# A planner that no longer charges the matmul behind a turn, and new priorities for every stage

## The chip, the cores and the metric

The kernel runs on one core of one Trainium2 chip. The metric is the device time of one execution in microseconds (us). Three runs of the kernel before gave 891.21, 891.24 and 893.26 us, so the median is 891.24 us. Engines are named as the profile names them: PE is TensorE (PEld its weight load), DVE is VectorE, ACT is ScalarE, POOL is GpSimd, SP is SyncE, which issues most DMAs.

## The reference: what is computed

Attention of 4 batches with 8 heads each (sequence 1152, head size 64), with the queries averaged in pairs, followed by a low-rank mix over the sequence and an MLP with a residual:

```python
q_pool = q.reshape(B, H, S // 2, 2, D).mean(axis=3)            # 576 queries per head
scores = q_pool @ k^T / sqrt(D); attn = softmax(scores)
x = (attn @ v) -> [4, 576, 512]
u = x + ((x^T @ U) @ V)^T                                       # U [576, 32], V [32, 576]
out = u + relu(u @ w_ch1) @ w_ch2                               # 512 -> 2048 -> 512
```

The weights of the second part arrive as 64-bit floats and are decoded on the chip.

## The kernel before, in words

The program is not written in the order in which it runs. The functions `head(n)` (32 heads) and `tail(b, clock)` (4 batches) record operations into a `Plan` with `op(at, ways, r, w, ...)`: `at` is a priority (a due time in ns), `ways` names the engines that may do it and a cost in ns on each, `r` and `w` are the buffers read and written. `Plan.run` then goes through all operations once, always giving the next free engine the earliest startable operation in order of due time, and emits the instructions in the order found. The costs and due times therefore decide only the order on each engine, the buffer slots and, for operations recorded with `dual` (L404), whether DVE or POOL does them. On the chip the engines then run these fixed queues with semaphores between them.

A head consists of these steps (lines of the kernel before):

- Loads of q, k, v by SP; the pooled query `qp` (L528, a dual operation); for batches 0 and 1 a split of k into a rounded half and the rest (L541 on ACT, L542 dual).
- Turns: transposes on PE into a PSUM bank of the pool `m` (5 banks): `qT` (L552, 3 fp32 transposes), `kT` (L630, 3 fp32r transposes, three such operations for a head of batches 0 and 1), or for batches 2 and 3 `kTw` (L585: one operation of 4 and one of 1 fp32 transposes).
- Scan: 14 matmuls per head (L657 of 384 columns, L659 of 288) into `m` banks, each followed by a DVE maximum over the bank (L663). The row maxima (L668) are turned by `mT` (L686, one fp32r transpose).
- Scores: 18 pairs of matmuls (L717 and L718) into the pool `s` (3 banks), exponentials on ACT (L724), and 7 or 8 sums of the exponentials into `acc` (L700, dual).
- `value` (L749: 18 matmuls with fp32 operands, each shown as two records) and, for each second head, the total of the exponentials (`total`, L740) and the turns `t2`, `t4` (L773) and `t3` (L786).

A batch's tail is the mix (L832, L851, additions L853), turns of u (`tu`, L923, 4 fp32 transposes per block of rows, split into halves by ACT L932 and DVE L933), and the MLP: first layer L957, second layer L1072, additions into X on DVE (L1076). For the last batch the first layer is done with 7 products instead of 8 (`pair`, L1001) and its operands are made at L897 to L914. MLP matmuls are spread between the heads of the next batch by their due times (`MLP_START`, `MLP_RATE`); the first batch's weights are decoded on ACT, DVE and POOL (L433 to L441) and split (L882, dual).

The planner marks the operations that are turns, value products or totals as `short` (a name for "not one of the plain one-pass matmuls"). Its rule `TURN` says that a matmul that is not `short` starts 82 ns later if the operation before it on PE was `short`.

Of the kernel before, what the change touches and what calls it, by code (L numbers as in the profile page):

```python
# [10 lines left out]
F32R = mybir.dt.float32r  # L11
# [27 lines left out]
class Op:  # L39
    __slots__ = ("at", "ways", "bufs", "deps", "succ", "open", "way", "start", "end", "seq", "port", "short")  # L40


class Plan:
# [12 lines left out]
    TURN = 82.0  # L56
# [4 lines left out]
    def op(self, at, ways, r=(), w=(), port=False, short=False):  # L61

        o = Op()
        o.short = short
# [27 lines left out]
    def run(self, slack, bias, bias_from, link):  # L92
# [9 lines left out]
        lead = False  # L102
# [42 lines left out]
        def pick(e):  # L145

            found, first = [], None
            for at, seq, base, o in cand[e][:self.WINDOW]:
                t = max(base, free[e] + (self.TURN if lead and e == "pe" and not o.short else 0.0))
# [37 lines left out]
        while len(order) < len(self.ops):  # L187
# [15 lines left out]
            if e == "pe":  # L203
                lead = o.short
# [34 lines left out]
def kernel(  # L239
# [33 lines left out]
    QT, KS = -9.86, -10.24  # L273
    LEAD = 60000.0, 9000.0
# [4 lines left out]
    TSW, TOT, TSL = 257.0, 235.0, -108.0  # L279
    SUM, AV, YT = 0.8, 0.51, 0.8184  # L280
# [3 lines left out]
    KT, MX0, MXS = 0.79, -8.744, 3.819  # L284
# [120 lines left out]
    TP, TPR, MOVE = 89, 84, 130  # L405
# [107 lines left out]
    def head(n):  # L513
        op = plan.op if n < len(heads) - 4 else lambda at, ways, r=(), w=(), port=False, short=False: plan.op(at, ways, [*r, *arena], w, port, short)
# [39 lines left out]
        op(T(QT), ("pe", 194, qT), [qp, (Q1, "use"), (Q2, "use")], [pt], short=True)  # L554
# [21 lines left out]
        def turn_whole(part, j0, j1):  # L576
# [11 lines left out]
            op(at, ("pe", len(kt_blocks) * TP if len(kt_blocks) > 1 else 27, kT), [(kt, 0), (T1, "use")], [pt_], short=True)  # L588
# [34 lines left out]
        else:  # L623
            for c in range(3):
# [7 lines left out]
                op(T(QT + KT * c), ("pe", 262, kT), kk[c] + [(T1, "use")], [pt_], short=True)  # L632
# [15 lines left out]
        for p0, p1 in ((0, 3), (3, 5)) if n == 0 else ((0, 5),):  # L648
# [23 lines left out]
            if n == 0:  # L672
# [4 lines left out]
                op(at, ("pe", np_ * TPR, mT), [mx], [pt2], short=True)  # L677
# [8 lines left out]
            op(at, ("pe", 62, lambda mx=mx, pt2=pt2, np_=np_: nc.tensor.transpose(  # L686
                pt2.t[0:np_, 0:P].bitcast(F32R), mx.t[:, 0:np_], identr)), [mx], [pt2], short=True)
# [14 lines left out]
        for j in range(NJ):  # L702
            if j % 2 == 0:
                pair_ = j + 1 < NJ
                pu[j] = new("p2" if pair_ else "p1")
                if pair_:
                    pu[j + 1] = pu[j]
                    todo = [((j, j + 1), 0, NARROW, j), ((j,), NARROW, NQ, j + 0.9), ((j + 1,), NARROW, NQ, j + 1.441)]
                else:
                    todo = [((j,), 0, HALF, j), ((j,), HALF, NQ, j + 0.4171)]  # L710
# [438 lines left out]
```

## Time and profile before

| | |
|---|---|
| median of 3 runs | 891.24 us |
| the profiled execution | 891.29 us |
| its span in the trace | 889.5 us |
| granted PE clock over the span | 1.00 (2.4 GHz) |
| PE busy | 880.7 us (99%) |
| DVE busy | 733.5 us (82%) |
| ACT busy | 521.4 us (59%) |
| POOL busy | 224.1 us (25%) |

The profiled execution took 891.29 us, of which 1.79 us lie around the span. Busy PE time is made of overlapping records: each matmul is shown for longer than the distance to the next start. A late start is therefore read from the distance between two starts in the timeline, not from the busy share.

### The profile page before, as it was taken

Reading aid. Unit: us, or ns where it says so; the run is one execution under the profiler, and the core shown is the slowest. Engines: PE = TensorE matmul, PEld = TensorE weight load, DVE = VectorE, ACT = ScalarE, POOL = GpSimd, SP = SyncE. Lnnn points to the kernel's source line nnn. Section 1 sums busy time; section 2 is a strip of 40 time slices with the busy share of each in tenths; the row PEclk is TensorE's granted clock in tenths of the full one; section 3 lists DMA queues with packets and bytes.
Section 4 is the critical chain, followed back from the end, with each engine's and each line's share of the span. In section 5 each row is a group of like instructions: output and inputs, shape, how many; then the busy total and the mean of one; then the engine's idle time right before and its main releaser. Section 6 shows DMA issues by size and latency. Waiting matters only on the chain.

```text
span 889.5 us, 15636 instructions
## 1 busy us (share of the span) xinstructions
PE 880.7 (99%) x5597; PEld 723.2 (81%) x5597; DVE 733.5 (82%) x1481; ACT 521.4 (59%) x1183; POOL 224.1 (25%) x224
## 2 busy tenths in 40 slices
PE   9999999999999999999999999999999999999998
PEld 8787777778787777889888888888888778899987
DVE  8899999988999989968786778787875554798885
ACT  6788889847787787655554657556564321322221
POOL 3323334434433455330213121200102000101110
PEclk9999999999999999999999999999999999999999
DMA  6244346345576664433332332324242255565432
GB/s 173 76 131 139 107 149 203 92 158 194 186 230 208 204 206 159 152 100 110 105 112 81 112 93 89 112 80 120 85 115 101 95 172 189 176 202 188 166 102 102
DMA packets 63635, 124.00 MB, mean 139 GB/s; under 512 B 5931, under 2 KB 33350, under 8 KB 63558
## 3 DMA queue, kind: packets, MB, share of 16 engines
q1 hardware_dynamic: 62214, 118.46, 41.2%
q10 hardware_dynamic: 1344, 4.56, 2.0%
q8 instruction: 44, 0.72, 0.4%
q14 instruction: 33, 0.27, 0.1%
HBM read 96.17 MB, written 21.50 MB: 132 GB/s over the span
## 4 chain that ended last, share of the span: by engine, by line
PE 87%; DVE 10%; ACT 1%; DMA 1%; issue 1%; POOL 0%; SPq 0%; DVEq 0%; POOLq 0%; ACTq 0%
PE m L1072 21%; PE m L957 16%; PE m L749 15%; PE s L717 7%; PE s L718 7%; PE m L657 7%; PE s L1001 6%; DVE mp L663 4%; DVE acc L700 2%; PE m L740 1%; PE m L630 1%; PE m L773 1%; PE m L585 1%; PE m L659 1%; PE m L552 1%; PE m L923 1%
## 5 line engine op out<-in xcount | busy, mean ns | idle before, releaser
L724 ACT ACTIVATE big<-s 128x320 f32<-128x320 f32 (+2 forms) x448 | 202.2, 479 | 104.9 <-PE s L718 101.2
L663 DVE TENSOR_REDUCE mp<-m 128x1 f32<-128x384 f32 (+1 forms) x448 | 214.5, 533 | 21.2 <-PE m L657 20.2
L1072 PE MATMUL m<-w,hh 128*128 128x512 f32 x798 | 221.2, 395 | 0.2 <-DVE XH L796 0.2
L957 PE MATMUL m<-rest,w 128*128 128x512 f32 (+1 forms) x768 | 180.5, 354 | 0.6 <-DVE mp L663 0.4
L717 PE MATMUL s<-room 128*128 128x256 f32 (+2 forms) x576 | 166.6, 301 | 0.3 <-ACT big L724 0.3
L1072 PEld LDWEIGHTS m<-w,hh 128*128 128x128 f32 x798 | 144.5, 188 | 25.8 <-DVE XH L796 0.4
L718 PE MATMUL s<-room 65*128 65x256 f32 (+2 forms) x576 | 164.5, 297 | 0.4 <-DMA room<-mr 0.4
L749 PE MATMUL m<-big,v 128*64 128x288 f32 x1152 | 148.5, 410 | 0.6 <-ACT mr L688 0.6
L957 PEld LDWEIGHTS m<-rest,w 128*128 128x128 f32 x768 | 131.5, 188 | 15.6 <-issue 1.3
L700 POOL TENSOR_TENSOR acc<-acc,big 128x576 f32<-128x576 f32 x67 | 95.7, 1428 | 156.1 <-ACT big L724 62.2
L700 DVE TENSOR_TENSOR acc<-acc,big 128x576 f32<-128x576 f32 x149 | 115.1, 773 | 13.2 <-ACT big L724 10.9
L657 PE MATMUL m<-room 128*128 128x384 f32 x384 | 124.7, 357 | 1.3 <-DVE mp L663 0.5
L749 PEld LDWEIGHTS m<-big,v 128*64 128x64 f32 x1152 | 79.1, 137 | 57.1 <-issue 2.1
L717 PEld LDWEIGHTS s<-room 128*128 128x128 f32 x576 | 109.0, 189 | 9.6 <-issue 2.2
L718 PEld LDWEIGHTS s<-room 65*128 65x128 f32 x576 | 108.9, 189 | 5.8 <-issue 0.5
L657 PEld LDWEIGHTS m<-room 128*128 128x128 f32 x384 | 69.3, 189 | 15.4 <-DVE mp L663 4.2
L1076 DVE TENSOR_TENSOR X<-m,X 128x512 f32<-128x512 f32 x95 | 64.7, 684 | 16.9 <-PE m L1072 16.6
L961 ACT ACTIVATE hh<-m 128x512 fp32r<-128x512 f32 (+1 forms) x64 | 33.0, 515 | 70.2 <-PE m L957 66.1
L397 ACT ACTIVATE room<-m 64x288 fp32r<-64x288 f32 (+1 forms) x173 | 72.4, 427 | 2.7 <-PE m L552 0.4
L963 DVE SCALAR_TENSOR_TENSOR hh<-m,hh 128x512 fp32r<-128x512 f32 (+1 forms) x64 | 37.5, 586 | 32.4 <-ACT hh L961 32.0
L565 POOL CAST qb<-room 64x64 fp32r<-64x64 f32 x57 | 17.5, 308 | 176.1 <-DVE acc L700 111.2
L441 POOL TENSOR_TENSOR wt<-wt,rx 128x512 int32<-128x512 int32 (+2 forms) x35 | 44.2, 1262 | 56.5 <-DVE w L882 11.6
(134 smaller groups left out, 1056.7 us busy)
## 6 DMA issues: line engine op xcount, KB each, us to landing
w<-wc SPq DMA_DIRECT2D x96, 512.0 KB
rx<-in_moe_w_ch_dram SPq DMA_DIRECT2D x32, 512.0 KB
wc<-w SPq DMA_DIRECT2D x32, 512.0 KB
q<-in_q_dram SPq DMA_DIRECT2D x32, 288.0 KB
v<-in_v_dram SPq DMA_DIRECT2D x32, 288.0 KB
k<-in_k_dram SPq DMA_DIRECT2D x31, 288.0 KB
room<-room ACTq DMA_DIRECT2D x15, 288.0 KB
out_dram<-X SPq DMA_DIRECT2D x11, 256.0 KB
```

What stands on the lines that cost most here:

```text
L397: ways = {"act": (a_(n, True) + hold, lambda: f(lambda o, i: nc.scalar.activation(o, i, AF.Copy)), far)}
L657: nc.tensor.matmul(pm.t[:, 0:w], Q1.t[:, t * P - 64:t * P + 64], T1.t[:, cs_], start=True, stop=True)
L663: op(T(MX0 + 0.3 + MXS * u / 14), ("dve", v_(w), lambda c=c, t=t, w=w, pm=pm: nc.vector.reduce_max(mp.t[:, c * 5 + t:c * 5 + t + 1], pm.t[ ...
L700: op(at, dual(NQ, lambda e: e.tensor_tensor(acc.t, a(), b_(), op=ALU.add)), r, [acc])
L717: nc.tensor.matmul(o, T1.t[:, kc], Q1.t[:, qa:qz], start=True, stop=False)
L718: nc.tensor.matmul(o, T2.t[:, kc], Q2.t[:, PAD + qa:PAD + qz], start=False, stop=True)
L724: op(T(when + 0.1), ("act", a_(len(js) * nq, True), lambda js=js, qa=qa, qz=qz, nq=nq, ss=ss, p=pu[j], e=js[0] % 2: nc.scalar.activation(p ...
L749: nc.tensor.matmul(pa.t[hf * D:(hf + 1) * D, 0:HALF], vt.t[:, j], pu[j].t[:, j % 2, hf * HALF:(hf + 1) * HALF], start=(j == 0), stop=(j == ...
L957: op(now, ("pe", mm(nb), lambda c=c, i=i, a=a, bb=bb, w=w, ph=ph, sl=sl: nc.tensor.matmul(ph.t[:, 0:nb], w.t[:, a, c * P:(c + 1) * P], (ul ...
L1001: nc.tensor.matmul(bank.t[:, 0:NB], left(a, c), ub.t[:, i, bb, c], start=(c == 0 and j == 0), stop=(c == 1 and j == 2))
L1072: op(now, ("pe", mm(512), lambda f=f, i=i, a=a, bb=bb, w=w, h_=h_: nc.tensor.matmul(po.t, h_.t[:, a, ns], w.t[:, bb], start=(f == fg and i ...
L1076: op(now, ("dve", v_(512), lambda: nc.vector.tensor_tensor(x(), po.t, x(), op=ALU.add)), [po], bk[t])
```

## The change

The field `short` and the 82 ns are removed from the planner. Operations that were marked `short` now carry a longer cost of their own: 276 would be 194 + 82, and `qT` is now 275; `kT` goes from 262 to 340, `mT` from 62 to 110, a single fp32 transpose from 89 to 109, `value` gains 83 and `total` 90. Further on, due times are set anew: those of the heads (`KS`, `SUM`, `AV`, `YT`, `MX0`, `MXS`, two offsets of the scores, `HEAD`), of the MLPs and of the decoding (`MLP_START`, `MLP_RATE`, `DEC_START`, `DEC_LEAD`, `LEAD`), the window within which the planner takes a more urgent operation before an earlier one (`SLACK`), and the bonus that DVE gets over POOL for dual operations (`BIAS`). The cost formula of POOL itself (`g_`) is as before. No instruction is added or removed on PE, DVE, ACT and POOL together: 4941 matmuls stand in both programs, and only their order, their banks and the engine of dual operations differ.

```diff
-    TURN = 82.0
...
-        lead = False
...
-                t = max(base, free[e] + (self.TURN if lead and e == "pe" and not o.short else 0.0))
+                t = max(base, free[e])
...
-            if e == "pe":
-                lead = o.short
...
-    QT, KS = -9.86, -10.24
-    LEAD = 60000.0, 9000.0
+    QT, KS = -9.86, -11.98
+    LEAD = 61900.5, 9797.53
...
-    TSW, TOT, TSL = 257.0, 235.0, -108.0
-    SUM, AV, YT = 0.8, 0.51, 0.8184
+    TSW, TOT, TSL = 340.0, 325.0, -190.0
+    SUM, AV, YT = 2.122, 0.6191, 0.79
...
-    KT, MX0, MXS = 0.79, -8.744, 3.819
+    KT, MX0, MXS = 0.79, -8.96, 3.655
...
-    HEAD0, HEAD = 16770.0, 21010.0
+    HEAD0, HEAD = 16770.0, 20929.9
...
-    MLP_START, MLP_RATE = 5.18, (2.2, 2.21, 2.18, 2.155)
-    DEC_START, DEC_LEAD = 102098.0, 12600.0
-    SLACK = 30.0
-    BIAS, BIAS_FROM = -330.1, 0.0
+    MLP_START, MLP_RATE = 5.443, (2.14, 2.192, 2.197, 2.194)
+    DEC_START, DEC_LEAD = 107967.0, 15253.3
+    SLACK = 27.8
+    BIAS, BIAS_FROM = -300.0, 0.0
...
-    TP, TPR, MOVE = 89, 84, 130
+    TP, TPR, MOVE = 109, 84, 130
...
-        op(T(QT), ("pe", 194, qT), [qp, (Q1, "use"), (Q2, "use")], [pt], short=True)
+        op(T(QT), ("pe", 275, qT), [qp, (Q1, "use"), (Q2, "use")], [pt])
...
-                op(T(QT + KT * c), ("pe", 262, kT), kk[c] + [(T1, "use")], [pt_], short=True)
+                op(T(QT + KT * c), ("pe", 340, kT), kk[c] + [(T1, "use")], [pt_])
```

Line numbers of the kernel after are 5 lower than those of the kernel before in everything that follows the planner.

**Place A: the turns of a head in batch 2, on PE.** This is the head whose `qT` starts at 441.89 us in the trace; `qp` and `k` are its query and key, `m_...` PSUM banks. Before:

```order
L717 MATMUL s_118<-room 128x288
L718 MATMUL s_118<-room 128x288
L552 MATMUL m_119<-ident,qp_79 128x96 x3
L585 MATMUL m_121<-ident,k_74 128x128 x4
L585 MATMUL m_122<-ident,k_74 64x128
L1072 MATMUL m_123<-w_3_110,hh_113 128x512
L1072 MATMUL m_120<-w_2_109,hh_115 128x512 x2
```

The three turns stand side by side, with plain matmuls on either side. Now, for the same head:

```order
L712 MATMUL s_118<-room 128x288
L713 MATMUL s_118<-room 128x288
L547 MATMUL m_119<-ident,qp_79 128x96 x3
L1067 MATMUL m_122<-w_3_110,hh_113 128x512
L1067 MATMUL m_121<-w_2_109,hh_115 128x512 x2
L580 MATMUL m_120<-ident,k_74 128x128 x4
L1067 MATMUL m_121<-w_2_109,hh_115 128x512
```

Plain matmuls stand between the turns, and the single transpose that ends the keys has moved out of this piece, to 11 rows behind the four.

**Place B: the start of the first MLP, on PE.** The turns of u (`X_98`) come before the first layer (`rest` times `w_0`); before:

```order
L923 MATMUL m_123<-ident,X_98 128x128 x4
L923 MATMUL m_119<-ident,X_98 128x128 x4
L717 MATMUL s_116<-room 128x288
L718 MATMUL s_116<-room 128x288
L923 MATMUL m_122<-ident,X_98 128x128 x4
L923 MATMUL m_120<-ident,X_98 128x128 x4
L657 MATMUL m_123<-room 128x384
L657 MATMUL m_119<-room 128x384
L657 MATMUL m_122<-room 128x384
L957 MATMUL m_120<-rest,w_0_104 128x512 x12
```

Only three scans stand between the last turn and the first layer. Now (a pair of scores, a total of four rows and one more scan are left out):

```order
L918 MATMUL m_119<-ident,X_98 128x128 x4
L918 MATMUL m_123<-ident,X_98 128x128 x4
L652 MATMUL m_120<-room 128x384
L712 MATMUL s_118<-room 128x256
...
L735 MATMUL m_121<-acc_82,ones 32x288
...
L625 MATMUL m_122<-identr,room 128x128 x3
L652 MATMUL m_119<-room 128x384
L712 MATMUL s_117<-room 128x320
L713 MATMUL s_117<-room 128x320
L652 MATMUL m_121<-room 128x384
L952 MATMUL m_123<-rest,w_0_104 128x512 x12
```

Three scans, six score matmuls, a total and a turn of keys now stand there.

**Place C: the first heads, on POOL.** `acc` are the sums of the exponentials `big`; `qp` and the row with `k` are the dual operations at a head's start, the casts belong to POOL in both. Before:

```order
L565 CAST qb_80<-room 64x64 x2
L528 TENSOR_TENSOR qp_79<-q_76 96x2x3x64
L542 TENSOR_TENSOR room<-k_75,room 128x9x64
L565 CAST qb_80<-room 64x64 x2
L528 TENSOR_TENSOR qp_79<-q_76 96x2x3x64
L542 TENSOR_TENSOR room<-k_74,room 128x9x64
L565 CAST qb_80<-room 64x64 x2
L700 TENSOR_TENSOR acc_82<-acc_82,big 128x576 x2
L542 TENSOR_TENSOR room<-k_75,room 128x9x64
```

Now, from the same cast on:

```order
L560 CAST qb_80<-room 64x64 x2
L523 TENSOR_TENSOR qp_79<-q_76 96x2x3x64
L537 TENSOR_TENSOR room<-k_75,room 128x9x64
L560 CAST qb_80<-room 64x64 x2
L523 TENSOR_TENSOR qp_79<-q_76 96x2x3x64
L695 TENSOR_TENSOR acc_81<-big 128x576
L695 TENSOR_TENSOR acc_81<-acc_81,big 128x576
L537 TENSOR_TENSOR room<-k_74,room 128x9x64
L560 CAST qb_80<-room 64x64 x2
L695 TENSOR_TENSOR acc_82<-big 128x576
L695 TENSOR_TENSOR acc_82<-acc_82,big 128x576
```

POOL now takes the first two sums of a head; over the whole program it does 25 of the 32 first sums instead of 8.

## Rows read from the trace of the kernel before

**Rows 1.** The page, part 1: busy us (share of span) and instructions.
```profile
PE 880.7 (99%) x5597; PEld 723.2 (81%) x5597; DVE 733.5 (82%) x1481; ACT 521.4 (59%) x1183; POOL 224.1 (25%) x224
```

**Rows 2.** Four stretches: length, busy time of each engine, granted clock, DMA share, GB/s.
```profile
core 0: us, PE busy (x) PEld busy (x) DVE busy (x) ACT busy (x) POOL busy (x), PEclk, DMA share, GB/s
27.00:160.00 133.00, 131.56 (x978) 101.85 (x977) 127.97 (x280) 115.09 (x271) 50.79 (x53) 1.00 0.46 133
160.00:365.00 205.00, 202.90 (x1231) 158.51 (x1230) 192.61 (x382) 151.95 (x331) 89.38 (x74) 1.00 0.56 182
365.00:700.00 335.00, 334.69 (x2225) 281.02 (x2226) 256.85 (x510) 192.41 (x458) 59.32 (x63) 1.00 0.33 104
700.00:870.00 170.00, 170.00 (x892) 145.73 (x889) 122.57 (x242) 44.29 (x87) 15.71 (x16) 1.00 0.49 168
```

**Rows 3.** The page, part 4: the chain that ended last, by engine.
```profile
PE 87%; DVE 10%; ACT 1%; DMA 1%; issue 1%; POOL 0%; SPq 0%; DVEq 0%; POOLq 0%; ACTq 0%
```

**Rows 4.** PE timeline, first late start after 27 us: start, length, instruction, idle before.
```profile
30.22 0.38 PE L717 MATMUL s<-room 128*128 128x256 f32 x1
30.97 0.36 PE L718 MATMUL s<-room 65*128 65x256 f32 x1 [0.37 <-DMA room<-mr]
31.16 0.28 PE L717 MATMUL s<-room 128*128 128x256 f32 x1
31.29 0.28 PE L718 MATMUL s<-room 65*128 65x256 f32 x1
```

**Rows 5.** PE timeline, last late start, at 622.19 behind two scans.
```profile
621.74 0.61 PE L657 MATMUL m<-room 128*128 128x384 f32 x2
622.19 0.31 PE L717 MATMUL s<-room 128*128 128x320 f32 x1
```

**Rows 6.** PE timeline at the start of the first MLP (place B).
```profile
177.72 1.04 PE L923 MATMUL m<-ident,X 128*128 128x128 f32 x8
178.76 0.44 PE L657 MATMUL m<-room 128*128 128x384 f32 x1
179.36 0.44 PE L657 MATMUL m<-room 128*128 128x384 f32 x1 [0.16 <-DVE rest L933]
179.96 0.44 PE L657 MATMUL m<-room 128*128 128x384 f32 x1 [0.16 <-DVE rest L933]
180.56 8.52 PE L957 MATMUL m<-rest,w 128*128 128x512 f32 x36 [0.16 <-DVE rest L933]
```

**Rows 7.** PE timeline, turns of a whole-key head side by side.
```profile
418.32 0.71 PE L585 MATMUL m<-ident,k 128*128 128x128 f32 x5
418.79 0.71 PE L1072 MATMUL m<-w,hh 128*128 128x512 f32 x2
419.34 0.28 PE L717 MATMUL s<-room 128*128 128x256 f32 x1
```

**Rows 8.** PE timeline, one transpose of the keys by itself.
```profile
351.62 0.27 PE L585 MATMUL m<-ident,k 128*64 128x128 f32 x1
351.64 0.48 PE L1072 MATMUL m<-w,hh 128*128 128x512 f32 x1
351.96 0.30 PE L717 MATMUL s<-room 128*128 128x320 f32 x1
```

**Rows 9.** PE timeline behind a value product, and a scan between plain matmuls.
```profile
448.94 0.61 PE L657 MATMUL m<-room 128*128 128x384 f32 x2
449.39 0.39 PE L1072 MATMUL m<-w,hh 128*128 128x512 f32 x1
449.62 0.34 PE L657 MATMUL m<-room 128*128 128x384 f32 x1
449.80 0.40 PE L1072 MATMUL m<-w,hh 128*128 128x512 f32 x1
```

**Rows 10.** PE timeline behind a turn of keys in fp32r.
```profile
253.69 0.35 PE L717 MATMUL s<-room 128*128 128x256 f32 x1
253.88 0.28 PE L718 MATMUL s<-room 65*128 65x256 f32 x1
254.01 0.28 PE L717 MATMUL s<-room 128*128 128x256 f32 x1
```

**Rows 11.** Groups of dual operations: busy, mean ns of one, idle before and releaser.
```profile
L700 DVE TENSOR_TENSOR acc<-acc,big 128x576 f32<-128x576 f32 x149 | 115.1, 773 | 13.2 <-ACT big L724 10.9 <-DVE mx L668 0.4 <-POOL acc L700 0.2
L882 DVE TENSOR_TENSOR w<-wt,w 128x512 fp32r<-128x512 f32 x25 | 17.0, 680 | 0.6 <-ACT w L881 0.5
L700 POOL TENSOR_TENSOR acc<-acc,big 128x576 f32<-128x576 f32 x67 | 95.7, 1428 | 156.1 <-ACT big L724 62.2 <-DVE mp L663 31.7 <-DVE X L1076 20.8
```

**Rows 12.** Waits of POOL: us in total, times, longest.
```profile
POOL qb L565 <- DVE acc L700: 111.2, 13, 24.2
```

More of the change, by code (lines that the diff above doesn't have):

```diff
@@ L39 @@
 class Op:
-    __slots__ = ("at", "ways", "bufs", "deps", "succ", "open", "way", "start", "end", "seq", "port", "short")
+    __slots__ = ("at", "ways", "bufs", "deps", "succ", "open", "way", "start", "end", "seq", "port")
 class Plan:
@@ L513, in head @@
     def head(n):
-        op = plan.op if n < len(heads) - 4 else lambda at, ways, r=(), w=(), port=False, short=False: plan.op(at, ways, [*r, *arena], w, port, short)
+        op = plan.op if n < len(heads) - 4 else lambda at, ways, r=(), w=(), port=False: plan.op(at, ways, [*r, *arena], w, port)
         b, h = heads[n]
@@ L587, in turn_whole @@
             at = T(QT + KT * (1 + part))
-            op(at, ("pe", len(kt_blocks) * TP if len(kt_blocks) > 1 else 27, kT), [(kt, 0), (T1, "use")], [pt_], short=True)
+            op(at, ("pe", len(kt_blocks) * TP, kT), [(kt, 0), (T1, "use")], [pt_])
             at += 0.6 * (T(1) - T(0))
@@ L755, in head @@
             op(T(j1 - 0.5 + AV), ("pe", n_ * 4 * (HALF / 2.4 + 1.0) + TSW + last * 138.0, value, TSL),
-               [(vt, 0)] + keys(range(j0, j1)) + (summed if last else []), [pa] + ([pk] if last else []), short=True)
+               [(vt, 0)] + keys(range(j0, j1)) + (summed if last else []), [pa] + ([pk] if last else []))
         op(T(NJ + AV), ("act", a_(HALF, True), lambda: nc.scalar.activation(ay.t[:, odd], pa.t[:, 0:HALF], AF.Copy)), [pa], [(ay, odd)])
@@ L761, in head @@
         if APART[b]:
-            op(T(NJ + AV), ("pe", parts * 4 * (HALF / 2.4 + 1.0) + TOT, total, TSL), summed, [pk], short=True)
+            op(T(NJ + AV), ("pe", parts * 4 * (HALF / 2.4 + 1.0) + TOT, total, TSL), summed, [pk])
         op(T(NJ + AV), ("act", a_(HALF, True), lambda: nc.scalar.activation(sr.t, pk.t[:, 0:HALF], AF.Copy)), [pk], [sr])
@@ L786, in t3 @@
                 nc.tensor.transpose(pz.t[:, t * P:(t + 1) * P], sr.t[:, c0:c0 + P], ident)
-        op(T(E), ("pe", 246, t3), [sr], [pz], short=True)
+        op(T(E), ("pe", 3 * TP, t3), [sr], [pz])
         op(T(E + 0.1), ("dve", 80, lambda: nc.vector.tensor_scalar_add(
             sm.t, pz.t[:, 0:3 * P].rearrange("p (c e x) -> p e c x", e=2, x=32)[:, :, :, 0], 1e-9)), [pz], [sm])
-        op(T(E), ("pe", 137, t2), [(ay, e) for e in range(2)], [pq], short=True)
-        op(T(E), ("pe", 4 * TP, t4), [(ay, e) for e in range(2)], [py], short=True)
+        op(T(E), ("pe", 2 * TP, t2), [(ay, e) for e in range(2)], [pq])
+        op(T(E), ("pe", 4 * TP, t4), [(ay, e) for e in range(2)], [py])
         op(T(E), ("dve", 135, lambda: nc.vector.reciprocal(rs.t, sm.t)), [sm], [rs])
@@ L925, in tail @@
             if quick:
-                op(max(now, clock - LEAD[0] + n * LEAD[1]), ("pe", 4 * TP, tu), bk[t], [pu], short=True)
+                op(max(now, clock - LEAD[0] + n * LEAD[1]), ("pe", 4 * TP, tu), bk[t], [pu])
                 operands(max(now, clock - LEAD[0] + n * LEAD[1]), n, pu)
                 continue
-            op(now, ("pe", 4 * TP, tu), bk[t] + [(uh, "use"), (ul, "use")], [pu], short=True)
+            op(now, ("pe", 4 * TP, tu), bk[t] + [(uh, "use"), (ul, "use")], [pu])
             o = slice(n * P, (n + 1) * P)
```

13 lines of the change are left out of this document (6 added, 7 removed).

## The prediction

> **What bounds the kernel now.** I read the shares first: PE is busy 99% of the span, DVE 82% [rows 1]. The chain that ended last says the same, 87% PE and 10% DVE, nearly nothing else [rows 3]. So the time is PE's work plus the moments at which PE starts late. By stretches [rows 2] there are two regimes. Up to 365 us DVE is almost as full as PE: 127.97 of 133 us (96.2%) and 192.61 of 205 (94.0%). From 365 to 700 us DVE has 256.85 of 335 (76.7%), and later 72%. The granted clock is 1.00 (2.4 GHz) in all four, so no term of mine is about it.
>
> The late starts come from the PE timeline. I took the usual distance between two starts for each kind of operation with its kinds of neighbours (the lower quartile of all its cases), and counted every start that comes over 0.09 us later. From 27 us on there are 69: 32 up to 160 us with 5.3 us in sum, 33 from 160 to 365 us with 7.0, 4 up to 700 us with 0.8, and none after. The first [rows 4] is 0.63 us late and waits for a DMA: 0.75 us pass between two starts that stand 0.13 apart in the next pair. The last [rows 5] has 0.45 us for two scans instead of 0.35. Most are scans that wait for a bank which DVE has not yet read. So 13.1 us is all that any new order can take away from the waits; the rest is PE's work and a fixed start.
>
> **The change part by part: PE.** The work itself is the same 4941 matmuls, but turns cost more when they are cut apart. I counted in both orders how often a plain matmul follows a turn, a value product or a total. Behind an fp32 turn: 50 times before, 92 now. Behind an fp32r turn: 34 and 51. Behind a value product or total: 20 and 35. Each kind has its price in the trace.
> - fp32 turns: side by side, five transposes take 0.47 us (418.32 to 418.79) and the two matmuls behind them 0.55, where one such matmul between plain ones takes 0.23 (449.39 to 449.62) [rows 7, 9]. The five at 0.109 each would be 0.545, so the last hands over 0.08 early and the matmul pays about 0.09. One transpose by itself and its matmul take 0.34 us (351.62 to 351.96) instead of 0.23 [rows 8]: again just its 0.109. A cut costs 0.005 us at most, 42 cuts 0.2 us. Place A is such a cut: it looks costly and is free.
> - fp32r turns: the matmul behind takes 0.19 us where its neighbour takes 0.13 [rows 10], so 0.06 times 17 cuts is 1.0 us.
> - value products and totals: two scans behind take 0.45 us, where one takes 0.18 between plain matmuls [rows 9], so 0.10 times 15 is 1.5 us.
>
> Sum +2.7 us. About 0.7 of it (33, 2 and 4 cuts) lies behind head 18, beyond 365 us, where PE never waits and nothing can hide it: that is the low end. The high end is 7.4 us (74 cuts at the dearest price). I take 2.7, because also before 365 us PE itself is what holds the chain most of the time.
>
> **DVE and POOL.** Of the dual operations, net 15 leave DVE for POOL: 8 sums (0.773 us each on DVE, 1.428 on POOL [rows 11]), 4 pooled queries, 4 weight splits (0.680 each [rows 11]), against 2 splits of k that go the other way; the rest is in the last batch's MLP, where no start is late. Up to 160 us (heads 1 to 9) net 8 operations leave DVE, 6.2 us at the price of a sum; place C shows it. From 160 to 365 us the first MLP's 4 weight splits and one net operation of the heads leave, 3.5 us. The saving in waits has two ends. At most all 13.1 us go. At least nothing goes, if the waits come from the order and not from DVE's load. Between them I take the stretches as three points: waits are 4.0% of the time with DVE at 96.2%, 3.4% at 94.0%, 0.24% at 76.7%, so about 0.185 points of waiting per point of DVE between the last two. The first stretch goes to 91.6% DVE (6.2 of 133 us less), so 2.9% waits: 1.4 us saved. The second goes to 92.3%: 0.7 us saved. Together -2.1 us, a value near the low end because the measured dependence is flat until DVE is far emptier.
>
> **The start of the first MLP** (place B). The scans at 178.76, 179.36 and 179.96 stand 0.60 apart instead of 0.18: 1.3 us lost while ACT and DVE split the turned blocks [rows 6]. The first-layer matmul comes 1.96 us after the last turn (177.72 plus eight at 0.109, to 180.56). The new order puts 2.4 us of scores, a total, a turn and scans there, at their usual distances, which covers the chain: -1.3 us. If DVE takes the scans' maxima ahead of the splits, the cover is gone and the wait stays. In the second and third MLP the new order leaves 2.0 and 1.9 us of work at this place where 8 and 20 us stood before. The chain of 1.96 us just fits: I add +0.3 us, bounded by 0 and by twice the 1.3 us seen here.
>
> Loads keep their issue order except for lead times; the DMA share is 0.33 to 0.56 [rows 2] and the only late start by a DMA of any size is the one in [rows 4]. I take 0 for them.
>
> Sum against the profiled execution: 891.29 + 2.7 - 2.1 - 1.3 + 0.3 = 890.9 us, 0.34 under the median of 891.24 (0.05 of that is the profiled run's own place). That is no change: a measurement of this kernel can tell 0.3%, 2.7 us, from none.
>
> **Rivals.** *The waits follow DVE's load one to one.* If DVE is truly the bound up to 365 us, each us that it sheds comes off: 6.2 + 3.5, and the 1.3 of the first MLP, so 891.29 + 2.7 - 11.0 = 883.0. For it: DVE at 96%, and scans as the usual late starts. Against it: PE's busy share there is as high, and PE takes on 2.0 us of turn costs in the same stretch, so it becomes the bound before all is shed. Its likely place is half way, 886.
>
> *POOL's longer operations hold up DVE.* This ends slower. A sum that moves occupies POOL for 1.428 us instead of DVE for 0.773 [rows 11]. The two take turns at operations of this kind: POOL waited 111.2 us behind DVE's sums [rows 12], and the program itself makes a POOL operation wait for the DVE one before it. From 160 to 365 us POOL is busy 89.38 us and DVE 192.61, together more than the 205. If what moves there (5 operations) and up to 160 us (8) delays DVE by the extra 0.655 us each, that is +8.5; with +2.7 for the turns and no saving 902.5, and with half of it on the chain 898. It decides once DVE waits for POOL longer than the 2.1 us that I count as saved; now it waits 0.2 us there [rows 11], which speaks against it. The same case holds the milder outcome that only the turn costs arrive, 894.0.
>
> The Trainium skill ("SBUF — State Buffer", section "SBUF: two separate sides") says that VectorE operations with two SBUF inputs and GpSimd operations share one port pair as an exclusive lock, where the loser blocks for the whole instruction; "Perfetto Trace Analysis" (section "Optimizing Scalar/DVE Operations") adds that moving work between the two might therefore not help. By that rule the gain of 2.1 us would be lost and the sum would be 893.0. The waits of POOL behind DVE agree with it, the 0.2 us of DVE behind POOL do not show it in the direction that would cost time here.
>
> *The change does not do what it says.* The words speak of other durations for POOL, yet its cost formula is untouched; what moves work to POOL is the bonus of DVE in the choice, 330.1 before and 300 now. Since the orders differ on all engines from the first heads on, an unchanged program is excluded, and this has no chance of its own.
>
> **How the numbers follow.** No change (888.6 to 893.9): 0.39, its own range being the bounds of the turn costs around 890.9. Faster (waits follow DVE's load): 0.35, 882 to 888.5. Slower (POOL in the way, or the turn costs without a saving): 0.26, 894 to 902. The range of 8 in 10 runs from 884, leaving out the full one-to-one case, to 898, leaving out POOL's full price.
>
> **What would show it.** Right: the timeline of PE shows turns in single pieces with a matmul 0.06 to 0.10 us longer behind fp32r turns and value products, and none longer in sum behind fp32 ones; the sums on DVE fall from 173 to 165; DVE's busy share up to 160 us falls by 3 to 5 points; the scans before the first MLP stand 0.18 us apart; beyond 365 us PE takes about 0.7 us more. Wrong: late starts up to 365 us under 6 us in sum (then DVE was the bound), DVE waiting for POOL by more than 2 us, or a new wait of over 1 us at one of the MLP starts or before the last batch's products.

## The result, and the profile after

The kernel after took 897.09 us in the median (896.74 to 897.33, 4 runs); the kernel before, on the same chip, 891.98. The ratio is 1.0056, 95% interval 1.0038 to 1.0073: slower by 5.1 us, where no change (890.9) was forecast. The profiled execution took 896.89 us with a span of 895.1, so 5.6 us more than the one of before.

The page, part 1 (answers to [rows 1]):

```profile
PE 884.5 (99%) x5597; PEld 722.9 (81%) x5597; DVE 736.0 (82%) x1466; ACT 525.4 (59%) x1181; POOL 243.1 (27%) x241
```

The four stretches, columns as in [rows 2]:

```profile
27.00:160.00 133.00, 131.44 (x975) 101.49 (x974) 127.24 (x273) 112.86 (x269) 58.03 (x57) 1.00 0.45 133
160.00:365.00 205.00, 201.63 (x1218) 157.51 (x1217) 191.83 (x370) 153.18 (x326) 95.35 (x82) 0.99 0.57 183
365.00:700.00 335.00, 335.00 (x2216) 278.65 (x2215) 257.35 (x511) 194.35 (x457) 62.10 (x66) 1.00 0.33 102
700.00:870.00 170.00, 169.35 (x883) 143.88 (x883) 121.93 (x239) 45.28 (x90) 15.89 (x17) 1.00 0.48 165
```

POOL took work over: 50.79 to 58.03 us up to 160 us. DVE did seven operations fewer there (280 to 273), but its busy time fell by only 0.73 us (127.97 to 127.24). The groups of dual operations (answer to [rows 11]) show why:

```profile
L695 DVE TENSOR_TENSOR acc<-acc,big 128x576 f32<-128x576 f32 x158 | 128.0, 810 | 19.3 <-ACT big L719 16.1 <-ACT room L392 0.5
L695 POOL TENSOR_TENSOR acc<-acc,big 128x576 f32<-128x576 f32 x58 | 82.8, 1428 | 103.0 <-ACT big L719 61.1 <-DVE mp L658 12.7 <-DVE rx L795 12.3
L695 POOL TENSOR_TENSOR acc<-big 128x576 f32<-128x576 f32 x25 | 35.6, 1426 | 102.1 <-ACT big L719 76.6 <-DVE X L1071 8.0 <-ACT room L596 6.8
L877 DVE TENSOR_TENSOR w<-wt,w 128x512 fp32r<-128x512 f32 x21 | 16.3, 777 | 0.5 <-ACT w L876 0.5
```

All first sums of DVE are gone but seven, as place C let expect, and the sums on DVE fell from 173 to 165 as forecast. But those left take 810 ns instead of 773, the weight splits 777 instead of 680. Fifteen sums on DVE are longer than 0.8 us, against seven before.

Each of the fifteen starts while an operation of POOL with two operands is running, and none of these is a sum: five times it is a pooled query, four times a split of k, six times a step of the decoding (before: two, two and three). The longest, from the timelines of DVE and POOL:

```profile
67.64 1.89 DVE L695 TENSOR_TENSOR acc<-acc,big 128x576 f32<-128x576 f32 x1
67.49 1.42 POOL L537 TENSOR_TENSOR room<-k,room 128x576 fp32r<-128x576 f32 x1
```

POOL's operation has 1.27 us left when the sum starts, and the sum takes 1.89: it ends 0.62 us after POOL's, and so do all fifteen (0.61 to 0.62). What the long sums take beyond 0.76 us each adds up to 9.2 us on DVE, against 3.2 before.

The longest waits of PE (engine, line, waited for: us in total, times, longest):

```profile
PE m L846 <- DVE xs L839: 2.8, 2, 2.1
PE s L484 <- DVE rest L407: 1.2, 1, 1.2
PE s L712 <- ACT big L719: 0.7, 1, 0.7
```

The first row is new: L846 is the mix of a batch (L851 before). (The second row is there before too: 1.2 us at L489.) The PE timeline around it (answer to [rows 6]):

```profile
164.66 2.84 PE L744 MATMUL m<-big,v 128*64 128x288 f32 x22
167.42 0.39 PE L712 MATMUL s<-room 128*128 128x256 f32 x1
...
168.01 0.52 PE L652 MATMUL m<-room 128*128 128x384 f32 x2
170.67 0.97 PE L846 MATMUL m<-xs,Vst 128*128 128x512 f32 x3 [2.14 <-DVE xs L839]
...
176.83 0.42 PE L652 MATMUL m<-room 128*128 128x384 f32 x1
...
178.57 0.41 PE L652 MATMUL m<-room 128*128 128x384 f32 x1
...
179.11 0.36 PE L652 MATMUL m<-room 128*128 128x384 f32 x1
179.31 2.92 PE L952 MATMUL m<-rest,w 128*128 128x512 f32 x12
```

The last lines are place B: the scans no longer wait, and the first layer starts 0.20 us behind the last one. But 2.14 us are lost at the mix ahead of it. Followed back, on DVE, ACT and SP:

```profile
169.93 0.68 DVE L839 TENSOR_TENSOR xs<-tr,xs 32x512 fp32r<-32x512 f32 x1 [2.64 <-ACT xs L837]
```
```profile
169.27 0.63 ACT L837 ACTIVATE xs<-tr 128x512 fp32r<-128x512 f32 x1 [2.55 <-DMA tr<-tr]
```
```profile
164.16 1.24 SPq L836 DMA_DIRECT2D tr<-tr  x2
```

The copies of `tr` leave SP at 164.16 and their data are used at 169.27. PE has a value product and 0.6 us of scores and scans for it, then nothing. In the kernel before the same copies and the first matmuls of the mix stand at:

```profile
167.73 1.25 SPq L841 DMA_DIRECT2D tr<-tr  x2
173.29 0.96 PE L851 MATMUL m<-xs,Vst 128*128 128x512 f32 x2
```

There PE is busy in between with scores, scans, a total and turns, and the data are used at 171.12, 3.4 us behind the issue instead of 5.1. The packets in the two traces show where the longer way comes from. The copies are 64 packets of 2048 bytes. In after 62 of them have landed by 166.87; the other two start at 167.89 and 168.11 and end at 168.34. From 166.43 to 167.91 a packet of 16384 bytes is on its way in one of the queues that the page marks "instruction", a load of instructions. The second wait at the mix has the same picture: an instruction packet from 728.13 to 729.61, and packets of the copies that start from 729.60 on. Before, the nearest instruction packet is over at 166.55, ahead of the copies. Without the two late packets the data would have been there about 1.5 us earlier, by these times; no run moved the instruction load alone.

What the clock did behind the wait (columns as in [rows 2]):

```profile
168.00:170.00 2.00, 0.53 (x4) 0.20 (x2) 0.07 (x1) 0.73 (x2) 0.00 (x0) 1.00 0.76 231
170.00:172.00 2.00, 1.33 (x6) 1.20 (x7) 1.94 (x4) 0.69 (x2) 0.45 (x1) 0.90 0.08 30
172.00:174.00 2.00, 2.00 (x9) 1.84 (x8) 2.00 (x4) 0.93 (x3) 1.78 (x2) 0.50 0.00 0
174.00:176.00 2.00, 2.00 (x13) 1.85 (x12) 1.69 (x4) 1.77 (x4) 1.98 (x2) 0.75 0.00 0
```

After the wait the granted clock is 0.50 (1.2 GHz) for some 3.4 us, with PE busy all the time. Three of the four executions have a mean granted clock of 0.998 over the span, which 3.4 us at half the clock make; the fourth has 1.000 and took 896.74 us. So the loss is there without the half clock too.

**Where the 5.6 us are.** I divided both PE timelines as in the forecast: the usual distance of each start from the one before it (by kind and neighbours, taken from the trace of before), and the rest. The usual distances sum to 858.0 us before and 860.9 after: **+2.9**, the order alone. The rest is 26.9 and 29.5: **+2.7**. In it late starts went from 3.7 to 4.0 us up to 27 us, from 5.3 to 6.3 up to 160, from 7.0 to 6.6 up to 365, from 0.8 to 1.0 up to 700 and from 0 to 0.9 behind it; the other 0.6 us are deviations too small to count. Between 160 and 365 us two things cancel: from the first mix matmul to the first layer the late starts rose from 2.1 to 4.0 us, elsewhere they fell from 4.9 to 2.6.

The division is an estimate: it depends on which neighbours are taken together. One stretch can be compared without it. From the turn of head 19's maxima (393.6 us before) to the last matmul 3002 records of PE take 492.4 us before, and 3003 take 495.6 after: **+3.1 of the 5.6 us**, where PE hardly waits. Late starts make about 1.1 of them.

### The profile page after: what moved, and what is told of

The parts are those of the page before. It is cut to its first block, busy times and chain, and to the rows that moved or that the text cites. A ratio compares the mean times of both kernels' runs of the same rounds, so it can differ in the third digit from the quotient of the medians.

```text
span 895.1 us, 15675 instructions
## 1 busy us (share of the span) xinstructions
PE 884.5 (99%) x5597; PEld 722.9 (81%) x5597; DVE 736.0 (82%) x1466; ACT 525.4 (59%) x1181; POOL 243.1 (27%) x241
## 4 chain that ended last, share of the span: by engine, by line
PE 86%; DVE 10%; DMA 1%; ACT 1%; issue 1%; SPq 0%; POOL 0%; DVEq 0%; ACTq 0%; POOLq 0%
PE m L1067 20%; PE m L952 15%; PE m L744 14%; PE s L712 8%; PE s L713 7%; PE m L652 7%; PE s L996 6%; DVE mp L658 3%; DVE acc L695 1%; PE m L735 1%; PE m L768 1%; PE m L580 1%; PE m L827 1%; PE m L625 1%; PE m L918 1%
## 5 line engine op out<-in xcount | busy, mean ns | idle before, releaser
L1067 PE MATMUL m<-w,hh 128*128 128x512 f32 x798 | 225.3, 397 | 0.0
L952 PE MATMUL m<-rest,w 128*128 128x512 f32 (+1 forms) x768 | 187.1, 356 | 0.1
L712 PE MATMUL s<-room 128*128 128x256 f32 (+2 forms) x576 | 169.2, 305 | 0.8 <-ACT big L719 0.7
L695 DVE TENSOR_TENSOR acc<-acc,big 128x576 f32<-128x576 f32 x158 | 128.0, 810 | 19.3 <-ACT big L719 16.1
L712 PEld LDWEIGHTS s<-room 128*128 128x128 f32 x576 | 109.7, 191 | 10.6 <-issue 4.4
L695 POOL TENSOR_TENSOR acc<-acc,big 128x576 f32<-128x576 f32 x58 | 82.8, 1428 | 103.0 <-ACT big L719 61.1
L695 POOL TENSOR_TENSOR acc<-big 128x576 f32<-128x576 f32 x25 | 35.6, 1426 | 102.1 <-ACT big L719 76.6
L958 DVE SCALAR_TENSOR_TENSOR hh<-m,hh 128x512 fp32r<-128x512 f32 (+1 forms) x64 | 37.4, 585 | 22.3 <-ACT hh L956 21.8
```

What stands on the lines that cost most here:

```text
L695: op(at, dual(NQ, lambda e: e.tensor_tensor(acc.t, a(), b_(), op=ALU.add)), r, [acc])
L712: nc.tensor.matmul(o, T1.t[:, kc], Q1.t[:, qa:qz], start=True, stop=False)
L952: op(now, ("pe", mm(nb), lambda c=c, i=i, a=a, bb=bb, w=w, ph=ph, sl=sl: nc.tensor.matmul(ph.t[:, 0:nb], w.t[:, a, c * P:(c + 1) * P], (ul ...
L1067: op(now, ("pe", mm(512), lambda f=f, i=i, a=a, bb=bb, w=w, h_=h_: nc.tensor.matmul(po.t, h_.t[:, a, ns], w.t[:, bb], start=(f == fg and i ...
```

## The experiments

The table holds, for each kernel that was planned or changed as a whole: the ratio to before with its interval, PE's usual distances against before, and the rest of the time from its first to its last start (26.9 us in before).

| run | ratio | usual, us | rest, us |
|---|---|---|---|
| after | 1.0056 [1.0038, 1.0073] | +2.9 | 29.5 |
| e1_planner_only | 1.0066 [1.0053, 1.0080] | +2.9 | 30.5 |
| e2_prio_only | 1.0123 [1.0109, 1.0137] | -0.1 | 38.0 |
| e3_mix_late | 1.0039 [1.0027, 1.0052] | +2.9 | 28.1 |
| e4_bias_back | 1.0026 [1.0016, 1.0036] | +2.9 | 26.4 |
| e6_short_pool_after | 1.0037 [1.0023, 1.0052] | +2.9 | 26.5 |
| e7_short_pool_before | 0.9988 [0.9979, 0.9997] | 0.0 | 27.5 |
| e8_true_costs | 1.0021 [1.0012, 1.0030] | +1.6 | 27.4 |
| e11_engines_before | 1.0085 [1.0068, 1.0101] | 0.0 | 32.7 |
| e12_engines_after | 1.0158 [1.0143, 1.0172] | +2.9 | 38.3 |
| e13_cut_rv_whole | 1.0153 [1.0134, 1.0172] | +2.2 | 37.4 |
| e14_cut_plain_whole | 1.0065 [1.0052, 1.0078] | +0.9 | 33.3 |
| e15_sum_only | 1.0012 [1.0001, 1.0022] | +0.1 | 28.4 |
| e16_sum_back | 1.0044 [1.0031, 1.0057] | +2.8 | 28.5 |

**One part alone.** e1 is the planner and costs of after with all due times of before (`SLACK` and `BIAS` too); e2 the planner of before with all due times of after. Of e1's edit against after:

```diff
-    SUM, AV, YT = 2.122, 0.6191, 0.79
+    SUM, AV, YT = 0.8, 0.51, 0.8184
...
-    BIAS, BIAS_FROM = -300.0, 0.0
+    BIAS, BIAS_FROM = -330.1, 0.0
```

> The planner without the charge and with the new costs, but all due times, SLACK and BIAS of the kernel before. Its order has 86 plain matmuls behind fp32 turns, 51 behind fp32r turns and 37 behind value products or totals (before: 50, 34, 20; after: 92, 51, 35). Theory T1 (cut turns cost 0.005, 0.06 and 0.10 us each, and waits are a matter of the priorities): about 2.9 us over the kernel before, and PE's usual distances show it. Theory T2 (the loss is in waits that the new priorities make, cuts are hidden): within 1 us of the kernel before.

> The planner of before with its charge and its costs, but all new due times, SLACK and BIAS. Its order has 55, 36 and 23 matmuls behind the three kinds of turns. T1: turn costs within 0.5 us of the kernel before; what remains of the 5.1 us is waits that the new priorities make, so 0 to 3 us over before. T2: nearly the whole loss, 4 to 5 us over before.

897.84 and 902.8 us against 892.2: +5.6 and +10.6, outside what either theory gave. The planner alone brings the whole +2.9 us of usual distances, and 3.6 us of rest. The due times alone bring none of the distances, and 11 us of rest: they suit only the planner that they came with.

**The wait at the mix.** e3 tells the planner that the copy of `tr` lands 2.5 us later, so it puts other work ahead of the mix:

```diff
-    ... nc.sync.dma_start(tr()[c * R:(c + 1) * R], tr()[0:R]), 175), [(trow, 0)], [(trow, c)])
+    ... nc.sync.dma_start(tr()[c * R:(c + 1) * R], tr()[0:R]), 175, 2500.0), [(trow, 0)], [(trow, c)])
```

> The kernel after, with one number more: the planner counts 2.5 us more for the two small copies in the mix of each batch (tr to tr), so that it puts more work on PE ahead of the matmuls that wait for them. T1 (the wait of 2.1 us at the first mix and the half clock behind it are 3 to 4 us of the loss, and the 0.8 us at the last mix too): 3 to 4.5 us faster than the kernel after, with the granted clock at 1.00 throughout. T3 (that wait only moves work about, since DVE is full there): within 1 us of the kernel after.

895.82 us, 1.3 less than after and not the 3 to 4.5 expected. From the mix to the first layer the late starts fall from 4.0 to 1.3 us and the clock stays at 1.00; but one new wait stands at the first layer itself:

```profile
181.69 3.48 PE L952 MATMUL m<-rest,w 128*128 128x512 f32 x14 [0.83 <-DVE rest L928]
```

The wait was real; about half of its price came back elsewhere. (In this trace too the last two packets of the copies start from 169.82 on, where an instruction packet ends, at 169.83; here PE has other work.)

**The bonus of DVE.** e4 is after with the old bonus:

```diff
-    BIAS, BIAS_FROM = -300.0, 0.0
+    BIAS, BIAS_FROM = -330.1, 0.0
```

> The kernel after with the bonus of DVE over POOL put back to 330.1. Theory T4 (POOL's sums hold up DVE's: 15 sums on DVE took over 0.8 us in the kernel after, 7 before): fewer long sums on DVE and 1 to 2 us faster than the kernel after. T1: as the kernel after within 1 us, but for what its other order happens to do at the mix.

894.52 us. The first MLP's mix no longer waits (four of its matmuls run in one piece; a value product ahead of it waits 1.0 us for ACT instead), and the rest of the span is at the level of before:

```profile
169.27 1.20 PE L846 MATMUL m<-xs,Vst 128*128 128x512 f32 x4
```

What is left, 2.3 us over before, is near what the usual distances add. The sums on DVE hardly shortened (803 ns, 14 of them long), so their length was not what made this difference: the plan around the mix fell out another way. The copies' last packet ends at 166.72 here, and the instruction packet starts at 170.88, behind them.

**Prices by themselves.** e5 is a small program of its own: 32 turns or value-like products and 32 plain matmuls, eight by eight and one by one; then 24 sums on DVE alone and 24 with POOL adding beside it. The reference's computation is left out.

```diff
+        for n in (8, 1):
+            for _ in range(32 // n):
+                for _ in range(n):
+                    turn()
+                for _ in range(n):
+                    plain()
```

> No attention and no MLP: on PE 32 turns of a kind and 32 plain matmuls of 512 columns, first in groups of 8 and 8, then one by one, for fp32 transposes, fp32r transposes and a fp32 product of 288 columns in turn; then on DVE 24 sums of 576 columns alone, 24 more while POOL does 24 sums of its own, and 24 maxima over a bank beside POOL. T1: one by one costs 28 cuts times 0.00 to 0.01 us more for fp32 transposes, 28 times 0.06 (1.7 us) for fp32r ones, 28 times 0.1 to 0.2 (2.8 to 5.6 us) for the products. T4 (POOL's sums hold up DVE's): DVE's sums take 0.75 us alone and 1 us or more beside POOL, with POOL's at 1.43 or longer; the maxima stay at 0.55. Without T4: 0.75 in both.

One by one instead of eight by eight cost 10.96 instead of 10.86 us for fp32 transposes (0.004 us a cut), 11.02 instead of 10.22 for fp32r (0.03) and 33.62 instead of 24.24 for fp32 products of 288 columns (0.34). The order of the kinds is as forecast, fp32r is half its price there, the products three times theirs. A DVE sum took 759 ns alone and 1870 beside POOL's, POOL's 1824 instead of the 1428 of the kernel. The ends alternate: DVE's sum ends 0.62 us after POOL's (29.04 and 29.66), POOL's next 1.28 us after DVE's (30.94), so a pair takes 1.90 us. The maxima of the program ran behind POOL's sums, so it says nothing on those.

**POOL's share.** In e6 (after) and e7 (before) sums that run on POOL cover 16 of 576 columns; those sums are left out of the result, the order and engines stay.

```diff
+            cols = lambda e: slice(0, 16 if e is nc.gpsimd else NQ)
```

> The kernel after in its own order, but each sum that POOL does covers 16 columns instead of 576 (these sums are left out of the result), so that POOL's operations are short and DVE's are not held up by them. T4: no sum on DVE over 0.8 us, DVE's busy time falls by about 9 us, and the time falls by 2 to 4 us. T1: under 1 us, since PE's turns and the wait at the mix stay.

> The same on the kernel before. T4: 7 long sums instead of 15, so it falls by 1 to 2 us, and the distance between this kernel and the same edit on the kernel after is 2 us smaller than the 5.1 us of the two whole kernels. T1: the distance stays 4 to 5 us.

894.92 and 890.91 us against 892.72. With POOL's sums at 219 ns in both, after is still 4.0 us slower than before, instead of 5.1: a difference of 1.1 us, which the intervals of the ratios do not tell from none. It prices POOL's sums alone. Long sums on DVE did not vanish (12 of 165, all beside other POOL operations), so what those cost is not in it. The mix still waits (again the last two packets of the copies start from 166.80 on, where an instruction packet ends), but in the execution that was profiled the clock stayed at 1.00 for the whole span:

```profile
169.64 0.97 PE L849 MATMUL m<-xs,Vst 128*128 128x512 f32 x3 [2.18 <-DVE xs L842]
```

**Charging the right turns.** e8 keeps the due times of before and charges the matmul only behind fp32r turns, value products and totals, with 109 ns for a transpose:

```diff
-    TP, TPR, MOVE = 89, 84, 130
+    TP, TPR, MOVE = 109, 84, 130
...
-        op(T(QT), ("pe", 194, qT), [qp, (Q1, "use"), (Q2, "use")], [pt], short=True)
+        op(T(QT), ("pe", 250, qT), [qp, (Q1, "use"), (Q2, "use")], [pt])
```

> The kernel before with its due times and its charge of 82 ns, but the charge only behind fp32r turns, value products and totals; fp32 transposes get 109 ns each and no charge, which is what the traces show. 1.6 us of PE's usual distances more than the kernel before (8 value products and 11 fp32r turns more stand by themselves), instead of 2.9. T1: 1.6 us over the kernel before, and less where waits shrink because PE's times are planned as they are; T2: nothing to be gained, waits decide, -3 to +5.

894.45 us. (The expectation counted 11 more fp32r turns than before; the order has 3 more of them, and 8 more value products and totals.) Against e1, which differs only in the charges, the profiled execution is 4.4 us shorter: 1.3 of usual distances and 3.1 of the rest.

**Cutting turns with nothing else changed.** In e9 and e13 the next plain matmul is pulled in between two turns behind fp32r turns, value products and totals of the kernel before; in e10 and e14 behind fp32 turns.

```diff
+            if kind(a) in self.CUT and kind(b) != "m":
+                ...
+                order[lo:hi + 1] = rest + turns
```

> The kernel before, with its own costs, due times and engines. Only this differs: where an fp32r turn, a value product or a total is followed by another turn, the next plain matmul is pulled in between. Plain matmuls then stand behind 51 fp32r turns instead of 34 and behind 40 value products and totals instead of 20. T1 (cut turns cost PE time that nothing hides): by the prices of the forecast 17 x 0.06 + 20 x 0.10 = +3.0 us, by the usual distances of the trace of before +2.4 us; waits within 1 us of those of before. T2 (where PE waits anyway the longer matmul only fills the wait, so part is hidden): +1 us or less. T3 (what costs is the new order of all else, not the cuts): within 0.5 us of before.

> The same as the run before it, but only behind fp32 turns: plain matmuls follow 103 of them instead of 50, everything else as in before. The forecast (a cut behind an fp32 turn is free, 0.005 us at most): 53 cuts cost +0.3 us. By the usual distances of the trace: +0.9. Rival (all kinds of turn cost the same, as the planner of before had it, 0.08 us): +4.3 us.

> As e9_cut_rv, without what spoiled that run: there six of the turns were pushed behind the load of the next tenant of the buffer that they read, so they waited for it (and turned a later head's data). These places are left as before now. A plain matmul stands behind 14 more fp32r turns and 20 more value products and totals than in before; order of all else, engines, costs and due times as before. T1 (cut turns cost PE time that little hides): 14 x 0.06 + 20 x 0.10 = +2.8 us by the forecast's prices, +2.2 by the usual distances of the trace of before; waits within 1 us of before. T2 (PE waits anyway, the longer matmul fills the wait): +1 us or less. T3 (the cuts are not what costs): within 0.5 us of before.

> As e10_cut_plain without the twelve turns that were pushed behind the load of their buffer's next tenant there. A plain matmul follows 97 fp32 turns instead of 50. The forecast (free, 0.005 us at most): +0.2 us. By the usual distances: +0.9. Rival (0.08 us a cut, as the planner of before charges): +3.8 us.

e9 and e10 say nothing on the price (918.94 and 922.71 us): a few turns were pushed behind the load of their buffer's next tenant, waited up to 3.1 us for it and turned a later head's data. Without those places e13 took 905.8 us (+13.4) and e14 898.3 (+5.9): both far over their numbers, and again by waits, since a pulled matmul is not always ready. In e13:

```profile
PE s L751 <- DMA room<-mr: 5.6, 5, 1.3
PE m L687 <- ACT room L427: 2.3, 3, 1.8
```

So none of the four isolates the price over the whole program. One part of e14 comes close: from head 19 on, where PE seldom waits, 27 more fp32 turns are cut; the time from the turn of head 19's maxima to the last matmul is 494.2 us instead of 492.4. Of the 1.7 us 1.0 are late starts; the 0.7 that remain are 0.03 us a cut, not 0.005. In e13 the same stretch has one more fp32r turn and three more value products or totals cut, and takes 492.4 us as before.

**DVE's load.** e11 and e12 keep the order of before (after) and exchange the engines of the dual operations in heads 1 to 9:

```diff
+            o.way = "pool" if o.seq in self.TO_POOL else "dve" if o.seq in self.TO_DVE else o.way
```

> The kernel before with its order; only the dual operations of heads 1 to 9 run on the engine that the kernel after gives them: 20 go from DVE to POOL and 8 the other way (10 sums, 2 pooled queries and 4 weight splits net to POOL, 4 splits of k to DVE). The forecast's term (DVE's load sets the waits up to 160 us): 1.4 us or a little more comes off. T1 (the waits come from single places of the order, not from DVE's load): within 0.5 us of before. Rival (POOL's longer sums hold up what reads them and DVE beside them): +1 to +4 us, with DVE sums longer than 0.8 us more often than the 7 of before.

> The kernel after with its order; only the dual operations of heads 1 to 9 run on the engine that the kernel before gives them: 20 go back from POOL to DVE and 8 the other way. The forecast's term: the relief is lost, 1.4 us or a little more slower than after. T1 (order): within 0.5 us of after; the wait before the mix at 170.7 stays at 2 us and more. Rival (POOL in the way): 1 to 3 us faster than after, fewer long sums on DVE than 15, late starts from 27 to 160 us back to about 5.3 us from 6.3.

899.98 us (+7.4) and 905.86 (+13.3, 8.8 over after). Both are slower, by more than any of the expectations had, so an assignment and its order belong together, and the pair does not tell load from order. But in e11 DVE is emptier up to 160 us than in before and the late starts there are 7.4 us instead of 5.3:

```profile
27.00:160.00 133.00, 129.53 (x963) 99.88 (x962) 125.03 (x266) 112.47 (x264) 57.13 (x58) 1.00 0.46 133
```

e15 and e16 move the same sums by the one due time that does it, with the order planned for it: e15 in before, e16 undone in after.

```diff
-    SUM, AV, YT = 0.8, 0.51, 0.8184
+    SUM, AV, YT = 2.122, 0.51, 0.8184
```

> The kernel before planned anew with one number of the change, the due time of the sums (SUM 0.8 to 2.122). Of the 65 sums of heads 1 to 9 POOL then does 21 instead of 11, as in after; PE's usual distances stay (+0.08 us in sum). The forecast's relief term: DVE's load falls and 1.4 us or more of waits go: 890.5 to 891.5 against 892.5 in this batch. T1 (waits come from single places and from sums that stretch beside POOL; DVE's load is not what sets them): late starts from 27 to 160 us stay at 5.3 us or rise, 0 to +2 us in time. Rival (POOL in the way, by the price of 0.655 us a sum moved): +6 us.

> The kernel after planned anew with the sums' due time of before (SUM 2.122 back to 0.8): 10 of the 65 sums of heads 1 to 9 on POOL instead of 21. PE's usual distances +2.8 us against before, as in after. The forecast's relief term: the relief is lost, 1.4 us or more slower than after. T1: no slower than after by more than 0.5 us; with late starts of 27 to 160 us at 5 to 6 us; in all 894 to 897, since the turns' +2.8 us stay. Rival (POOL in the way): 2 us or more faster than after, and long sums on DVE back to about 7.

893.22 us (+0.9) and 896.28 (0.8 under after). Up to 160 us, e15 above and e16 below:

```profile
27.00:160.00 133.00, 131.13 (x984) 101.19 (x981) 125.10 (x275) 114.25 (x268) 59.27 (x58) 1.00 0.47 139
```
```profile
27.00:160.00 133.00, 130.35 (x963) 99.61 (x962) 127.80 (x278) 114.29 (x268) 46.14 (x48) 1.00 0.47 135
```

Ten sums more on POOL take 2.9 us of load from DVE and leave the late starts nearly where they were (5.1 against 5.3 us); the time does not fall. Undoing it in after puts only 0.6 us of load back on DVE, brings the long sums from 15 to 7, and does not cost. Neither run shows the relief term, as far as two orders planned anew can tell; POOL's full price (+6) is refuted.

No run here beat the kernel before with the whole computation done.

## Why the prediction was wrong

**The turn costs, +2.7: the sum came out, its parts did not.** The order adds +2.9 us of usual distances, and what these leave over (small deviations) agrees in both traces within 0.6 us. In the trace of after a value product is followed by three matmuls in 0.80 us, where three take 0.69, and a scan behind a turn of keys takes 0.25 instead of 0.18:

```profile
448.67 4.59 PE L744 MATMUL m<-big,v 128*64 128x288 f32 x36
453.19 0.96 PE L1067 MATMUL m<-w,hh 128*128 128x512 f32 x3
453.99 0.68 PE L652 MATMUL m<-room 128*128 128x384 f32 x3
...
259.77 0.37 PE L625 MATMUL m<-identr,room 128*128 128x128 f32 x3
259.98 0.41 PE L652 MATMUL m<-room 128*128 128x384 f32 x1
260.23 0.31 PE L712 MATMUL s<-room 128*128 128x320 f32 x1
```

But the forecast put 0.7 us of it beyond 365 us. From head 19 on, at 393.6 us, the order costs 3.1 us, of which late starts make about 1.1: some 2 us remain, three times as much, and then less than 1 us for all that lies before. The same order with POOL's sums short shows it again (e6 495.4 us, e7 492.2). A cut behind an fp32 turn is not free (0.03 us in e14, where the forecast had 0.005 at most), one behind an fp32r turn cost 0.03 in e5 instead of 0.06. That the sum is so near is in part luck. In the table usual distances and rest add up to the time by construction, so the runs whose rest is near that of before (e4, e8, e15) do not test the price. The edits that cut turns on purpose did not isolate it over the whole program either.

**The relief of DVE, -2.1: the first step that failed.** The forecast read waits as a function of DVE's share and took 6.2 us off that share up to 160 us. Neither held. DVE's load fell by 0.7 us there: the sums fell from 39.6 to 35.8 us, 3.8 less where ten fewer at 0.773 would have been 7.7 less, and three more splits of k came to DVE, at 954 ns each. Late starts rose from 5.3 to 6.3 us. From 160 to 365 us the load fell by 0.8 us instead of 3.5, and outside the first MLP 2.3 us of late starts went all the same, where the forecast had 0.7. And where the load did fall by 2.9 us (e15), nothing came back. The three points of share and waiting were three stages with different work, not one dependence.

The lines of these sums, up to 160 us, before and after (the first sums, 6.8 us before, are a line of their own):

```profile
L700 DVE TENSOR_TENSOR acc<-acc,big 128x576 f32<-128x576 f32 x43 | 32.8, 764 | 0.7 <-DVE mx L668 0.4
L695 DVE TENSOR_TENSOR acc<-acc,big 128x576 f32<-128x576 f32 x42 | 35.8, 852 | 1.0 <-ACT big L719 0.3
```

The Trainium skill ("SBUF — State Buffer", section "SBUF: two separate sides") has the lock between the two engines that I weighed and set aside because DVE waited only 0.2 us for POOL; e5 and the fifteen long sums agree with the rule. The cost does not show as a wait in the profile but as a longer operation, so neither the 0.2 us nor POOL's waits of [rows 12] bore on it. What the long sums cost PE is open: e6 and e7 shorten POOL's sums, and the long ones stand beside other operations of POOL.

I also named the wrong cause of the move: planned with the bonus 300 alone (no run was made of it), the order of before differs in two dual operations; the sums move by their due time (e15: POOL does 21 of the 65 sums of heads 1 to 9 instead of 11).

**The first MLP, -1.3: the second step that failed, and the larger.** The scans stand as forecast and the 1.3 us are gone. But the step asked only what covers the chain behind the turns of u. The chain ahead of them, from the copies of `tr` to the mix, lost its cover and got longer: 2.14 us of waiting, about 1.5 of them by the two late packets, and in the profiled execution half the clock for 3.4 us. From the mix to the first layer late starts rose by 1.9 us where -1.3 was forecast, 3.2 us of the 6.0 between forecast and profile. This was on the list of what would prove the forecast wrong (a new wait of over 1 us at an MLP start), but had no term and no price; "I take 0" for the DMAs looked only at the loads.

**Later starts, +0.3: the place was wrong.** The second and third MLP have no such wait; the last batch's mix has one of 0.7 us, and 0.9 us are late behind 700 us where nothing was.

**The rivals.** The measured time lies in the range of the slower case. Its mechanism, POOL holding up DVE at 0.655 us a sum, did not come: ten sums moved cost 0.9 us in e15. POOL did hold up DVE, but by its other operations, 9.2 us of longer sums instead of 3.2. What came is the milder form, the turn costs without a saving (894.0), and 2.7 us more of rest: 1.9 more at the mix, 1.0 up to 160 us, 0.9 behind 700 us and about 1.2 in small parts, less the 2.3 that went between 160 and 365 us. How the bonus, 30 ns in the planner, removes the wait at the mix (e4) can't be told in full: many operations change places at once, and the instruction load no longer meets the copies.

## What to carry to other kernels

When a new order is weighed, walk every chain that crosses engines and a DMA at a stage's seam, and count the work that stands beside it now: a wait that leaves one place of the seam can stand ahead of it afterwards. Look at the packets of a small copy on such a chain: one late packet holds back the whole copy. Look for an engine's holdups in the length of its operations, not only in its waits. Don't read a price per point of load from stages that do different work. A planner's costs and due times are one setting: each alone, and each engine assignment on a foreign order, was slower here by 6 to 13 us.

## What was not expected of the hardware

- A wait of 2.1 us at the mix was followed by the half clock in after (0.50 from 171.6 to 175.0 us), and a wait of 2.2 us at the same place in e6 was not. It is not the kernel alone that decides: of after's four executions one has a mean clock of 1.000, and of e6's seven four have 1.000 (894.0 to 894.9 us) and three 0.996 to 0.998 (896.9 to 898.8). What sets it is open.
- The last two of the 64 packets of the copies started only where an instruction packet of 16384 bytes ended: the first of them at 167.89 us and that end at 167.91 in after, 166.80 and 166.80 in e6, 169.82 and 169.83 in e3. That the one holds up the other is read from these times, not tested.
- An fp32 product of 288 columns, cut from its like, cost 0.34 us more in e5, while behind a value product in the kernel a plain matmul is only 0.11 us late. Why they differ was not tried.
- DVE's sum beside POOL's took 1870 ns instead of 759, more than twice, and POOL's 1824 instead of the kernel's 1428: with both at it, DVE shows no idle time, and both stretch. In the kernel after, a sum that started beside another operation of POOL ended 0.62 us behind it, whether 0.27 or 1.27 us of that were left.
